# Fillers of half the columns in bank 6 and up to a later time, four result buffers in the first pass, and the place of the later sums split in two

## The chip, the cores and the metric

The kernel runs on one core of one Trainium2 chip. The metric is the device time in microseconds (us) of one execution; the median of the runs counts. The five engines of the core that the text names are TensorE (PE in the profile, with PEld for its weight loads), VectorE (DVE), ScalarE (ACT), GpSimd (POOL) and SyncE (SP), whose queue issues the DMA transfers.

## The reference

Attention over a window of 128 positions with a linear bias, in 8 batches of 8 heads (576 positions, 64 dimensions each), and a gated feed-forward layer on its 4608 tokens. All inputs are float32.

```python
scores = scale * np.matmul(q, k.transpose(0, 1, 3, 2))
rel = pos[:, None] - pos[None, :]
bias = slopes[:, None, None] * (-np.abs(rel).astype(np.float32))[None, :, :]
mask = (rel >= 0) & (rel < window)
scores = np.where(mask, scores + bias[None], -1000000000.0)
scores = scores - np.max(scores, axis=-1, keepdims=True)
attn = np.exp(scores)
attn = attn / (np.sum(attn, axis=-1, keepdims=True) + 1e-09)
x = np.matmul(attn, v)                         # then laid out as (4608, 512)
gate = 1.0 / (1.0 + np.exp(-(x @ w_gate)))     # w_gate, w_val: 512 x 1536
val = x @ w_val
out = gate * val @ w_out                       # 1536 x 512
```

## The kernel before, in words

The work is in three passes over the tokens. The first pass lies beside the attention: as soon as the tokens of a block of 512 are there, `ffn` computes 2 of the 12 chunks of 128 hidden units for them and stores the partial result to DRAM (`part`). Two more passes, with 5 chunks each, read the partial results back and add to them (`ffn2`, tokens in blocks of 768). Every operand of the feed-forward layer is split into a high and a low part of the type fp32r, and a product is three matmuls (high x high, low x high, high x low). The float32 weights are decoded from integer words by ScalarE (L299) and VectorE (L300, L303) before they are split (`prepare`, `prepare2`).

Attention goes through the eight PSUM banks `mm[0]` to `mm[7]` so: scores (L386) into banks 2 to 5, masking there by VectorE (L399), bias and maximum (L407), exponentials on ScalarE (L410), normalisation (L430, L431), transposes (L435) into bank 6, copies `both` from there (L181), a selection on GpSimd (L446), values (L472) into bank 7 and, for the last 64 columns, into the tail of bank 6, and copies `xt` of both (L181). The first pass has banks 0 and 1 for itself until the attention is nearly over, and all eight in its last two blocks.

The order of each engine is not the order of the code: every operation is put into a graph with an engine, a planned cost and keys that it reads and writes, and `order` plays a list schedule. An operation of the kind `copy` or `minus` may go to one of two engines. Where the planner sees a gap ahead of an operation on PE that starts before `WARM`, it fills it with calls of `warm` (L246), matmuls whose result nobody reads, as many as the gap holds at a price written into `order`. The tile framework adds the waits that the use of the same tile asks for; an operation of ScalarE on bank 6 thus waits for an earlier matmul into bank 6, whatever its columns.

`project_out` multiplies the hidden units by `w_out` (L559), and ScalarE copies the result into a buffer `ob` (L567) from which SP's queue stores it; in the later passes VectorE adds the partial result `pi` instead (L564). In the second and third pass a chunk is seven products (L660) of sums of the token block, `combo(0)` to `combo(6)`, with sums of the weights; the banks are combined through `a1`, `u2` and `p5` (L667, L675). The sums of the tokens take the place `area`, in which the first pass has its split tokens and its weights, all but the lower half of `w_out`: that has a place of its own, `area_o`, which the sum `s1` takes over. `follow` puts an empty operation into the graph that makes the listed keys wait for each other at the change of passes.

## Time and profile before

| | |
|---|---|
| runs | 1047.24, 1048.8 and 1049.0 us, median 1048.8 |
| profiled execution | 1052.11 us, of which 1050.4 are its span |
| PE busy | 1030.6 us, 98% of the span |
| VectorE, ScalarE, GpSimd busy | 731.5, 529.0, 110.7 us |
| granted clock of TensorE, mean | 0.997 |
| first pass and attention | 0 to about 360 us |
| second and third pass | from about 360 us to the end |

Times in the rows are counted from the first instruction of the span. A granted clock of 1.00 is TensorE's higher level of 2.4 GHz, 0.50 the lower of 1.2 GHz. A float32 matmul of the program shows as two records in the trace.

### The profile page before, as it was taken

The numbers are of one execution on the slowest core, as the hardware profiler recorded it, in microseconds if no ns is written. First come the engines' busy times: TensorE is split into PE (matmuls) and PEld (weight loads), VectorE is DVE, ScalarE is ACT, GpSimd is POOL, SyncE is SP. The second block draws the span as 40 slices with busy tenths as digits, with TensorE's granted clock in tenths as the row PEclk, the third lists the DMA queues.
The fourth block names the chain that finished last, engine by engine and source line by source line (L and its number), as shares of the span: only waits on it lengthen the run. The fifth ranks groups of instructions, "written<-read, shape, count | busy, mean of one in ns | idle before, by whom it ended". The sixth has DMA issues, their size and how long they took to land.

```text
span 1050.4 us, 17342 instructions
## 1 busy us (share of the span) xinstructions
PE 1030.6 (98%) x6024; PEld 915.9 (87%) x6024; DVE 731.5 (70%) x2045; ACT 529.0 (50%) x1466; POOL 110.7 (11%) x205
## 2 busy tenths in 40 slices
PE   9899999999998999999999999999999999999998
PEld 7577778878877898989999998989898999999896
DVE  8998788798878776474747475999647474747352
ACT  6898688787855542433424152645243342415140
POOL 2333233343310000000000000010000000000000
PEclk9999999999999999999999999999999999999999
DMA  8758576857455715032220405362403223050303
GB/s 290 247 191 278 187 236 212 303 169 263 162 177 181 238 61 158 23 100 81 86 95 26 155 1 181 100 200 82 151 31 106 75 68 113 9 172 1 120 1 100
DMA packets 74727, 142.68 MB, mean 136 GB/s; under 512 B 7312, under 2 KB 30224, under 8 KB 74640
## 3 DMA queue, kind: packets, MB, share of 16 engines
q1 hardware_dynamic: 74640, 141.58, 40.7%
q8 instruction: 47, 0.77, 0.3%
q14 instruction: 40, 0.33, 0.1%
HBM read 103.81 MB, written 37.75 MB: 135 GB/s over the span
## 4 chain that ended last, share of the span: by engine, by line
PE 90%; DVE 5%; ACT 3%; DMA 1%; issue 1%; POOL 0%; ACTq 0%; DVEq 0%; POOLq 0%
PE mm L660 42%; PE mm L559 26%; PE mm L522 8%; PE mm L472 5%; PE mm L386 5%; PE mm L435 3%; ACT pb L410 1%; DVE first L190 1%; PE mm L246 1%; DMA wraw<-in_moe_w_out_dram 1%; DMA wraw<-in_moe_w_gate_dram 1%; ACT both L181 1%; DVE wbits L303 0%; DVE mm L399 0%; DVE w2s L190 0%
## 5 line engine op out<-in xcount | busy, mean ns | idle before, releaser
L660 PE MATMUL mm<-later,w2s 128*128 128x384 f32 x2160 | 386.6, 335 | 1.6 <-ACT later L181 1.3
L660 PEld LDWEIGHTS mm<-later,w2s 128*128 128x128 f32 x2160 | 377.3, 188 | 3.4 <-ACT later L181 1.7
L559 PE MATMUL mm<-w2o,hidden 128*128 128x512 f32 x1080 | 249.2, 390 | 0.0
L559 PEld LDWEIGHTS mm<-w2o,hidden 128*128 128x128 f32 x1080 | 202.4, 188 | 40.8
L671 ACT ACTIVATE sg<-mm 128x384 f32<-128x384 f32 x120 | 59.0, 492 | 149.2 <-PE mm L660 99.4
L181 ACT COPY a<-mm 128x384 f32<-128x384 f32 x60 | 28.8, 480 | 196.1 <-PE mm L660 192.8
L446 POOL TENSOR_SCALAR_AFFINE_SELECT pt<-both 128x384 f32<-128x384 f32 x192 | 103.7, 563 | 183.2 <-ACT both L181 160.7
L522 PE MATMUL mm<-first 128*128 128x512 f32 x432 | 113.2, 405 | 2.6 <-ACT ob L567 2.5
L564 DVE SCALAR_TENSOR_TENSOR ob<-mm,pi 128x512 f32<-128x512 f32 x72 | 49.5, 689 | 73.3 <-PE mm L559 40.0
L522 PEld LDWEIGHTS mm<-first 128*128 128x128 f32 x432 | 78.9, 191 | 20.2 <-ACT ob L567 4.1
L667 DVE TENSOR_TENSOR mm<-mm,a 128x384 f32<-128x384 f32 x60 | 33.7, 564 | 79.3 <-PE mm L660 79.3
L410 ACT ACTIVATE pb<-pb,st 128x128 f32<-128x128 f32 x216 | 84.6, 398 | 3.1 <-DVE st L407 2.9
L660 PE MATMUL mm<-xc,w2s 128*128 128x384 f32 x360 | 73.0, 337 | 0.4 <-DVE p L667 0.4
L472 PEld LDWEIGHTS mm<-pt,vr 128*64 128x64 f32 x832 | 61.2, 137 | 12.6 <-issue 9.5
L472 PE MATMUL mm<-pt,vr 128*64 128x256 f32 (+2 forms) x832 | 67.4, 306 | 0.6 <-POOL pt L446 0.6
L660 PEld LDWEIGHTS mm<-xc,w2s 128*128 128x128 f32 x360 | 63.6, 188 | 1.7 <-DVE p L667 0.7
L181 ACT COPY both<-mm 128x384 f32<-128x384 f32 x94 | 44.8, 477 | 34.3 <-PE mm L435 22.4
L399 DVE COPY_PREDICATED mm<-early_h,mm 128x256 f32<-128x256 int32 (+1 forms) x144 | 49.1, 392 | 9.7 <-PE mm L386 9.3
L386 PE MATMUL mm<-kr,qr 64*128 64x256 f32 (+1 forms) x396 | 55.3, 383 | 0.0
L559 PE MATMUL mm<-first,early_h 128*128 128x512 f32 x144 | 52.4, 409 | 2.2 <-DVE early_h L190 2.0
L407 DVE CUSTOM_DVE_ANT_0 pb<-mm,early_h 128x128 f32<-128x128 f32 x216 | 51.3, 280 | 0.0
L667 DVE TENSOR_TENSOR mm<-mm,u 128x384 f32<-128x384 f32 x60 | 33.9, 565 | 19.8 <-PE mm L660 19.8
(112 smaller groups left out, 1287.7 us busy)
## 6 DMA issues: line engine op xcount, KB each, us to landing
part<-ob SPq DMA_DIRECT2D x72, 256.0 KB, 3.7
pi<-part SPq DMA_DIRECT2D x72, 256.0 KB, 3.4
later_xr<-xs SPq DMA_DIRECT2D x16, 768.0 KB, 5.1
kr<-in_k_dram SPq DMA_DIRECT2D x21, 576.0 KB, 5.4
vr<-in_v_dram SPq DMA_DIRECT2D x32, 288.0 KB, 3.4
xs<-xt SPq DMA_DIRECT2D x32, 288.0 KB, 3.0
out_dram<-ob SPq DMA_DIRECT2D x36, 256.0 KB, 2.1
qr<-in_q_dram SPq DMA_DIRECT2D x21, 320.0 KB, 5.8
```

The source lines that it names most:

```text
L181: g.add("ACT", act_cost(n, psum), lambda: nc.scalar.copy(out(), src()), reads, writes, want, release=release, ways=[("DVE", dve_cost(n, ps ...
L386: nc.tensor.matmul(sp[bank_of(r, a)][:, a % 2, lo:], qraw(u)[rows, i // 2], kraw(u)[rows, (i - 1) * P + lo:(i + 1) * P], start=True, stop= ...
L407: g.add("DVE", 0.21, lambda: nc.vector.tensor_tensor_reduce(pb()[:, e], sp[b][:, a, P:], relm[u.p][:, w], op0=ALU.add, op1=ALU.min, scale= ...
L410: g.add("ACT", 0.39, lambda: nc.scalar.activation(pb()[:, e], pb()[:, e], AF.Exp, bias=st()[:, e:e + 1], scale=-1.0, accum_out=st()[:, 3 + ...
L446: nc.gpsimd.affine_select(pt(u)[:, f0:f0 + 2 * n - 1:2, :], both(), [[0, n], step], cmp, 0.0, base=0, channel_multiplier=mult)
L472: nc.tensor.matmul(to()[e * D:(e + 1) * D, a - e * S - t0:b - e * S - t0], vraw(u)[:, c], seen, start=first, stop=last, skip_group_check=True)
L522: nc.tensor.matmul(mm[s], w.tile(kind, wi)[:, i, c * P:(c + 1) * P], x()[:, c, :], start=(k == 0 and c == 0), stop=(k == 2 and c == KC - 1))
L559: nc.tensor.matmul(mm[s], hcol(x, i, w is w1)[:, ts], w.tile("o", wi)[:, i, :], start=(i == 0 and k == 0), stop=(i == n - 1 and k == 2))
L564: g.add("DVE", dve_cost(DM, psum=True), lambda: nc.vector.scalar_tensor_tensor(ob(), mm[s], 0.5, pi(), op0=ALU.mult, op1=ALU.add), [("mm", ...
L660: nc.tensor.matmul(mm[b][:, 0:N2], w.tile2(i, wp)[:, wk, c * P:(c + 1) * P], combo(k, xp)[:, c], start=(start and c == 0 and j == 0), stop ...
L667: g.add("DVE", dve_cost(N2, psum=True), lambda: nc.vector.tensor_tensor(o(), bk(b)(), a(), op=ALU.add), [("mm", b), *reads] if okeys else ...
L671: g.add("ACT", act_cost(N2, psum=True), lambda: nc.scalar.activation(sg[h](), bk(b)(), AF.Tanh, scale=0.5), [("mm", b)], [("sg", h)], F)
```

## The change

Five things change. The planner fills gaps up to 80 us where it stopped at 30, and counts a filler at 0.13 us (0.23 ahead of 5 us) where it counted 0.25 (0.45). The filler has 64 moving columns and writes the last 64 columns of bank 6, where it had 128 and wrote the first 128 of bank 1. The first pass uses four buffers `ob`, of which the third and the fourth share the place of the `pi` buffers of the later passes. The area is shorter by one weight half: both halves of the first pass's `w_out` are now in `area_o`, which later takes `combo(5)`, while `s1` moves to the pool of the later weights; and the empty operation at the change of passes is split, so that the sums 0 to 4 wait for the tokens and the two input weights, and `combo(5)` for `w_out`. Last, `a1` and `u2` have one buffer where they had two.

```diff
--- before.py
+++ after.py
@@ -44,7 +44,7 @@
 SLACK = 1.0
 W0, WSTEP = 20.0, 2.0
 SWITCH = 0.36
-WARM = 30.0
+WARM = 80.0
 YIELD = {"DVE": 0.1, "POOL": 0.0}
 NRAW = 2
 
@@ -119,7 +119,7 @@
                 mode = o.mode
                 o.start += SWITCH / 2
             if o.eng == "PE" and o.start < WARM:
-                gap = (o.start - free["PE"] - 0.2) // (0.25 if free["PE"] > 5.0 else 0.45)
+                gap = (o.start - free["PE"] - 0.2) // (0.13 if free["PE"] > 5.0 else 0.23)
                 if gap > 0:
                     self.fill.append((free["PE"] + 0.01, int(gap)))
             wait.remove(o)
@@ -243,13 +243,13 @@
 
     def warm(n):
         for _ in range(n):
-            nc.tensor.matmul(mm[1][:, 0:P], ident, ident, start=True, stop=True)
+            nc.tensor.matmul(mm[6][:, NB - D:], ident, ident[:, 0:D], start=True, stop=True)
 
     g.warm = warm
 
 
 
-    AREA = 2 * KC * NB + 5 * FC1 * DM
+    AREA = 2 * KC * NB + 4 * FC1 * DM
     area = lambda a, n, name="first": T(moe, name, [P, AREA], F32R, tag="area")[:, a:a + n]
 
     class First:
@@ -257,7 +257,8 @@
 
         def tile(self, kind, part_):
             a = 2 * KC * NB + (2 * "gvo".index(kind) + part_) * FC1 * DM
-            t = area(a, FC1 * DM) if a < AREA else T(moe, "first_o", [P, FC1 * DM], F32R, tag="area_o")
+            size = FC1 * DM
+            t = area(a, size) if kind != "o" else T(moe, "first_o", [P, 2 * size], F32R, tag="area_o")[:, part_ * size:(part_ + 1) * size]
             return t.rearrange("p (i f) -> p i f", i=FC1)
 
         def keys(self, i):
@@ -547,10 +548,11 @@
 
     def project_out(r, at, h, w, col, F):
         n, last = len(w.fcs), w.fcs[-1] == NFC - 1
-        s, o, ts = bank(), outs[0] % 2, slice(at, at + P)
+        many = 4 if w is w1 else 2
+        s, o, ts = bank(), outs[0] % many, slice(at, at + P)
         outs[0] += 1
         pi = lambda: T(moe, f"pi{o}", [P, DM], F32)
-        ob = lambda: T(moe, f"ob{o}", [P, DM], F32)
+        ob = lambda: T(moe, f"ob{o}", [P, DM], F32) if o < 2 else T(moe, f"ob{o}", [P, DM], F32, tag=f"pi{o - 2}")
         if w.fcs[0]:
             move(pi, lambda: part[r], [("part", r)], [("pi", o)], F, 256)
         for i in range(n):
@@ -579,7 +581,12 @@
 
     def combo(k, part_):
         n = 4 * N2
-        tile_ = area(k * n, n, "later") if k < ROOM else T(pools["w2"], f"xc{k}", [P, n], F32R)
+        if k < ROOM:
+            tile_ = area(k * n, n, "later")
+        elif k == ROOM:
+            tile_ = T(moe, "later_o", [P, 2 * FC1 * DM], F32R, tag="area_o")[:, 0:n]
+        else:
+            tile_ = T(pools["w2"], f"xc{k}", [P, n], F32R)
         return tile_.rearrange("p (h c t) -> p h c t", h=2, c=2)[:, part_]
 
 
@@ -621,7 +628,7 @@
                      [("xs", b, p) for p in range(NPAIR)], [("xr", k, (h, a % N2 > 0)) for k in range(2)], F, 2 * (e - a))
                 a = e
         xk = {(h, k): [("xr", k, (h, e)) for e in range(2)] for h in range(2) for k in range(2)}
-        s1 = lambda: T(moe, "later_s1", [P, FC1 * DM], F32, tag="area_o")[:, 0:2 * N2].rearrange("p (c t) -> p c t", c=2)
+        s1 = lambda: T(pools["w2"], "xsum1", [P, 2, N2], F32)
         s2 = lambda: T(moe, "xsum", [P, 2, N2], F32)
         m = 2 * N2
 
@@ -648,8 +655,8 @@
         def chunk(i):
             bx, by, bz = bank(), bank(), bank()
             e = i % 2
-            small = lambda x: T(pools["w2"], f"{x}{e}", [P, N2], F32)
-            a1, u2, p5 = (lambda x=x: small(x) for x in ("a1", "u2", "p5"))
+            small = lambda x: T(pools["w2"], x, [P, N2], F32)
+            a1, u2, p5 = (lambda x=x: small(x) for x in ("a1", "u2", f"p5{e}"))
             sg = [lambda h=h: T(moe, f"sg{h}", [P, NB], F32)[:, 0:N2] for h in range(2)]
             bk = lambda b: (lambda: mm[b][:, 0:N2])
 
@@ -679,7 +686,7 @@
                 minus(lambda: hcol("hl", i, False)[:, h * N2:(h + 1) * N2], val, lambda: as32(hi()), N2, keys + [("hh", i, h)],
                       [("hl", i, h)], F, psum=psum)
 
-            ka, ku, kp = (("a1", e), ("u2", e), ("p5", e))
+            ka, ku, kp = ("a1", "u2", ("p5", e))
             product(0, bx, True, 0)
             copy(a1, bk(bx), N2, [("mm", bx)], [ka], F, psum=True)
             product(3, bz, True, 3)
@@ -753,7 +760,10 @@
             def follow(keys):
                 g.add("PY", 0.0, lambda: None, [], keys, FIRST)
 
-            follow(tenants(0, 2 * AREA) + ["w2pool", "s1"] + [("xc", k, j) for k in range(7) for j in range(2)])
+            follow(tenants(0, AREA) + [("xc", k, j) for k in range(ROOM) for j in range(2)])
+            follow(tenants(AREA, 2 * AREA) + [("xc", ROOM, j) for j in range(2)])
+            follow(["w2pool", "s1", "a1", "u2", ("p5", 0), ("p5", 1)] + [("xc", k, j) for k in range(ROOM + 1, 7) for j in range(2)])
+            follow([("ob", o) for o in range(4)] + [("pi", o) for o in range(2)])
             follow([("xr", c, e) for c in range(KC) for e in range(2)] + [("xr", k, (h, e)) for k in range(2) for h in range(2) for e in range(2)])
             follow([(x, i, h) for x in ("hh", "hl") for i in range(FC2) for h in range(2)] + ["w2pool"])
         for t in range(NT2):
```

In the changed file L299 is L300, L386 is L387, L435 is L436, L472 is L473, L522 is L523, L559 is L561, L567 is L569 and L660 is L667.

The order of PE near the start, behind the first scores. `mm1` and `mm6` are PSUM banks, `ident` is the unit matrix. Before:

```order
L246 MATMUL mm1_141<-ident_71 128x128 x12
L435 MATMUL mm6_146<-ident_71,early_h2_148 128x128 [waits DVE_49] x3
L246 MATMUL mm1_141<-ident_71 128x128 x2
L386 MATMUL mm2_142<-kr0_150,qr0_152 128x256
L386 MATMUL mm4_144<-kr1_166,qr1_168 128x128 [waits DMAHW6_49,DMAHW5_49]
L386 MATMUL mm2_142<-kr1_166,qr1_168 128x256
```

After:

```order
L246 MATMUL mm6_146<-ident_71 128x64 x24
L436 MATMUL mm6_146<-ident_71,early_h2_148 128x128 [waits DVE_49] x3
L246 MATMUL mm6_146<-ident_71 128x64 x3
L387 MATMUL mm2_142<-kr0_150,qr0_152 128x256
L387 MATMUL mm4_144<-kr1_174,qr1_176 128x128 [waits DMAHW6_49,DMAHW5_49]
L387 MATMUL mm2_142<-kr1_174,qr1_176 128x256
```

The groups of fillers are longer and go to bank 6, into which the transposes between them write too. Over the whole program PE had groups of 8, 12, 2, 9 and 9 calls; it has groups of 16, 24, 3, 18, 18 and 17, the last behind the transposes of `early_h2` and in front of the values (L472) that start at 34.55 us in the trace before.

The order of ScalarE in the last block but two of the first pass, at the result copies. Before:

```order
L567 ACTIVATE ob0_1184<-mm0_140 128x512 [waits DMAHW6_49,PE_49]
L567 ACTIVATE ob1_1220<-mm1_141 128x512 [waits DMAHW0_49,PE_49]
L181 CAST w2o0_3755<-wbits1_400 128x512 [waits DVE_49]
L299 ACTIVATE wbits0_364<-wraw1_190 128x512 [waits DMAHW4_49,DVE_49,Activation_49]
L567 ACTIVATE ob0_1184<-mm0_140 128x512 [waits DMAHW5_49,PE_49,Activation_49]
L567 ACTIVATE ob1_1220<-mm1_141 128x512 [waits DMAHW6_49,PE_49,Activation_49]
```

After:

```order
L300 ACTIVATE wbits0_394<-wraw1_198 128x512 [waits DMAHW1_49,DVE_49]
L569 ACTIVATE ob0_1240<-mm0_140 128x512 [waits DMAHW2_49,PE_49,Activation_49]
L569 ACTIVATE ob1_1276<-mm1_141 128x512 [waits DMAHW4_49,PE_49,Activation_49]
L181 CAST w2o0_3814<-wbits1_439 128x512 [waits DMAHW7_49,DVE_49]
L569 ACTIVATE ob2_1345<-mm0_140 128x512 [waits DMAHW6_49,PE_49,Activation_49]
L569 ACTIVATE ob3_1420<-mm1_141 128x512 [waits DMAHW7_49,PE_49,Activation_49]
```

The decode into `wbits0` stood between the second and the third copy; it stands ahead of the first.

The order of PE at the change of passes: the last group of the last block of the first pass and the first products of the second pass. Before:

```order
L559 MATMUL mm7_147<-first_406,early_h0_1002 128x512
L559 MATMUL mm7_147<-first_o_955,early_h0_1002 128x512
L559 MATMUL mm7_147<-first_406,early_h1_1022 128x512
L660 MATMUL mm0_140<-later_3989,w2s00_2670 128x384 [waits Activation_49]
L660 MATMUL mm0_140<-later_3989,w2s01_2735 128x384
L660 MATMUL mm0_140<-later_3989,w2s00_2670 128x384 [waits DVE_49]
```

After, the end of the block before the last:

```order
L561 MATMUL mm7_147<-first_o_998,early_h0_1058 128x512 [waits Activation_49]
L561 MATMUL mm7_147<-first_o_998,early_h0_1058 128x512
L561 MATMUL mm7_147<-first_o_998,early_h1_1078 128x512
L667 MATMUL mm0_140<-later_4006,w2s00_2635 128x384 [waits Activation_49]
L667 MATMUL mm0_140<-later_4006,w2s01_2646 128x384
L667 MATMUL mm0_140<-later_4006,w2s00_2635 128x384 [waits DVE_49]
L667 MATMUL mm0_140<-later_4006,w2s00_2635 128x384
L667 MATMUL mm0_140<-later_4006,w2s01_2646 128x384
L667 MATMUL mm0_140<-later_4006,w2s00_2635 128x384
L561 MATMUL mm4_144<-first_o_998,early_h0_1058 128x512 [waits Activation_49]
```

The first six products of the second pass stood behind all of L559; now the whole last block of L561, whose first row is the last one here, follows on them.

## Rows read from the trace of the kernel before

**Rows 1.** The page: its head, the row of PE in part 1 (busy time, share of the span, instructions), and the shares by engine of the chain that ended last.

```profile
span 1050.4 us, 17342 instructions
...
PE 1030.6 (98%) x6024; PEld 915.9 (87%) x6024; DVE 731.5 (70%) x2045; ACT 529.0 (50%) x1466; POOL 110.7 (11%) x205
...
PE 90%; DVE 5%; ACT 3%; DMA 1%; issue 1%; POOL 0%; ACTq 0%; DVEq 0%; POOLq 0%
```

**Rows 2.** Two stretches: their length, busy time and records of each engine, the granted clock of TensorE, the DMA share and GB/s.

```profile
24.00:80.00 56.00, 50.65 (x398) 37.60 (x397) 52.97 (x266) 51.82 (x209) 20.70 (x36) 1.00 0.65 218
365.00:1050.00 685.00, 680.99 (x3583) 637.40 (x3581) 423.81 (x701) 254.44 (x507) 2.78 (x2) 1.00 0.27 89
```

**Rows 3.** What PE waited for between 20 and 100 us: us in total, times, longest.

```profile
PE mm L435 <- ACT both L181: 4.5, 8, 1.1
```

**Rows 4.** The same between 100 and 366 us.

```profile
PE mm L522 <- ACT ob L567: 2.5, 2, 1.8
PE mm L559 <- DVE early_h L190: 2.0, 2, 1.2
...
PE mm L660 <- ACT later L181: 1.3, 1, 1.3
PE mm L660 <- DVE later L190: 0.4, 1, 0.4
```

**Rows 5.** The two stretches of four microseconds behind late stalls, in the columns of rows 2 (the granted clock stands behind the busy times).

```profile
330.00:334.00 4.00, 4.00 (x12) 3.13 (x11) 2.48 (x5) 0.99 (x2) 0.00 (x0) 0.57 0.80 201
361.00:365.00 4.00, 4.00 (x16) 4.00 (x15) 4.00 (x6) 3.36 (x6) 0.00 (x0) 0.57 0.63 166
```

**Rows 6.** PE in order of time: start, length, line, tiles, shapes, records, and in brackets the idle time before them. L246 is the filler, L435 a group of transposes, L386 scores, L472 values.

```profile
1.42 3.78 PE L246 MATMUL mm<-ident 128*128 128x128 f32 x16 [1.42 <-POOL ident masks.py:199]
...
7.86 2.94 PE L246 MATMUL mm<-ident 128*128 128x128 f32 x24
10.64 0.49 PE L435 MATMUL mm<-ident,early_h 128*128 128x128 f32 x3
...
14.10 2.27 PE L246 MATMUL mm<-ident 128*128 128x128 f32 x18
16.21 0.56 PE L435 MATMUL mm<-ident,pb 128*128 128x128 f32 x3
...
17.24 0.60 PE L386 MATMUL mm<-early_h,early_xr 64*128 64x128 f32 x4
...
21.71 2.17 PE L246 MATMUL mm<-ident 128*128 128x128 f32 x18
...
34.55 1.08 PE L472 MATMUL mm<-pt,vr 128*64 128x256 f32 x6
36.20 1.12 PE L472 MATMUL mm<-pt,vr 128*64 128x256 f32 x8 [0.57 <-POOL pt L446]
```

**Rows 7.** Weight loads (PEld) and matmuls of the filler, loads of L472 (64 columns), with the shortest, median and longest duration in ns; and the first filler matmul of the second stretch in the timeline.

```profile
L246 PEld LDWEIGHTS mm<-ident x80: 186/192/333, 1.4 to 23.5; 128*128 128x128 f32 x80
L246 PE MATMUL mm<-ident x80: 275/275/580, 1.4 to 23.6; 128*128 128x128 f32 x80
...
L472 PEld LDWEIGHTS mm<-pt,vr x832: 132/137/138, 19.3 to 296.7; 128*64 128x64 f32 x167
...
7.86 0.38 PE L246 MATMUL mm<-ident 128*128 128x128 f32 x1
```

**Rows 8.** A weight load of the first scores, with what it waited for.

```profile
6.26 0.29 PEld L386 LDWEIGHTS mm<-kr,qr 64*128 64x128 f32 x2 [0.21 <-DMA kr<-in_k_dram]
```

**Rows 9.** VectorE and ScalarE beside these stretches, in order of time: copy_predicated on the scores (L399), and ScalarE's copies (L181) out of bank 6. The row at 22.18 holds both copies of `xt`; the second is of 64 columns from bank 6.

```profile
12.67 0.43 DVE L399 COPY_PREDICATED mm<-early_h,mm 128x256 f32<-128x256 int32 x1 [1.50 <-PE mm L386]
...
18.44 0.28 DVE L399 COPY_PREDICATED mm<-early_h,mm 128x128 f32<-128x128 int32 x1
...
22.18 0.67 ACT L181 COPY xt<-mm 128x512 f32<-128x512 f32 x2
...
35.09 0.46 ACT L181 COPY both<-mm 128x384 f32<-128x384 f32 x1
```

**Rows 10.** Part 6 of the page, stores of the partial results: issues, KB each, median us from issue to landing.

```profile
part<-ob SPq DMA_DIRECT2D x72, 256.0 KB, 3.7
```

**Rows 11.** Around 327 us: the issue of a `w_out` load on SP's queue, ScalarE's decode (L299) and result copies (L567), and PE behind them.

```profile
321.27 0.33 SPq L186 DMA_DIRECT2D wraw<-in_moe_w_out_dram  x1
...
327.75 0.66 ACT L299 ACTIVATE wbits<-wraw 128x512 f32<-128x512 f32 x1 [4.32 <-DMA wraw<-in_moe_w_out_dram]
328.47 1.24 ACT L567 ACTIVATE ob<-mm 128x512 f32<-128x512 f32 x2
...
329.13 2.40 PE L522 MATMUL mm<-first 128*128 128x512 f32 x7 [1.79 <-ACT ob L567]
```

**Rows 12.** The change of passes: ScalarE's first casts of the sums, PE behind them, and in two successive chunks the product that reads `xc` (L660).

```profile
358.65 1.55 ACT L181 CAST later<-later_xr 128x768 fp32r<-128x768 f32 x2
...
359.53 0.62 PE L660 MATMUL mm<-later,w2s 128*128 128x384 f32 x2 [1.27 <-ACT later L181]
...
382.65 1.22 PE L660 MATMUL mm<-xc,w2s 128*128 128x384 f32 x6
...
389.96 1.23 PE L660 MATMUL mm<-xc,w2s 128*128 128x384 f32 x6
```

**Rows 13.** Part 5 of the page: the copies of `a1`.

```profile
L181 ACT COPY a<-mm 128x384 f32<-128x384 f32 x60 | 28.8, 480 | 196.1 <-PE mm L660 192.8
```

## The prediction

> **What bounds the kernel now.** I read the page's shares first. TensorE (PE) is busy 1030.6 of 1050.4 us and carries 90% of the chain that ended last [rows 1]: the kernel is bound by PE almost everywhere, and from 365 us on there is nothing to gain, 680.99 of 685 us being busy at full clock [rows 2]. A change of buffers can then win only where PE stands still or runs at a lower clock, and it loses wherever it gives PE more to do. So next I asked the trace where PE waits. Between 20 and 100 us it waits mainly for ScalarE's copies `both` (4.5 us in eight waits) [rows 3]; between 100 and 366 us for the result copies `ob` (2.5 us), for `early_h` (2.0) and for the sums of the pass change (1.3 and 0.4) [rows 4]. Two of those stalls are followed by four microseconds at a granted clock of 0.57 [rows 5]: of the two levels, most of that stretch is at 1.2 GHz, and each costs 4 x (1 - 0.57) = 1.72 us on top of its wait. Everywhere else that I asked, the column is 1.00, from 24 to 80 us too [rows 2]. Last comes the filler, read as PE's instructions in order of time [rows 6]. One call of it shows as two records.
>
> **The filler, more calls.** The planner divides a gap by the price of one call; the price goes from 0.25 to 0.13 us (0.45 to 0.23 ahead of 5 us). The order gives 16, 24, 3, 18, 18 and 17 calls, 96 in all, where 8, 12, 2, 9 and 9 stood, 40 in all; the last, in front of `values` near 34.6 us, is new. What a call then costs is the question on which the sign rests. Today a record takes (10.64 - 7.86)/24 = 0.116 us in the second stretch and (16.21 - 14.10)/18 = 0.117 in the fourth, each time up to the transpose behind it [rows 6]. If its 128 moving columns set that, 64 columns take half, 0.058. If the load of its 128 x 128 weights sets it, the price does not fall. Two rows speak on the load. The first filler matmul of a stretch lasts 0.38 us where the median is 275 ns, so it stood 0.10 us for its own weights; and a load of 64 columns shows 137 ns where that of 128 columns shows 192, 55 ns for 64 columns, which makes 0.11 us for 128 [rows 7]. Both come to the 0.11 of a record. Every matmul record has a load record (80 and 80), so each would pay for one. I take 0.117 us a record: the load bounds it.
>
> The Trainium skill, "TensorE: Matmul & The Clock Gate", section "Back-to-back issue gap", gives the gap as N/2.4 + 2.5 ns; with two passes of 64 columns to a record that is an estimate of 56 ns, the halved price, but the section itself says that the formula undercounts at small N for want of the weight loads. By it the sum would be that of rival B; the rows of the loads decide against it here.
>
> **What that adds at the start.** Stretch by stretch, at 0.117 us a record:
> first: 16 more records, but here one took 3.78/16 = 0.236, twice as long [rows 6]. Halved exactly it costs nothing; unhalved 3.8, of which a wait for `kr` behind it (0.21 [rows 8]) would take a little. Nearer to nothing, since the half of 0.236 is still as long as a load: +0.6.
> second: 24 more, +2.8, all on the chain, for PE does nothing else from 7.86 to 10.64 and the scores behind it feed VectorE, which idles 1.50 us for them [rows 9].
> third: 2 more, +0.2.
> fourth: 18 more, 2.1 on PE, but VectorE wants the scores of 17.24 (0.60 long) only at 18.44 [rows 6, 9], so 0.6 is hidden: +1.5.
> fifth: 18 more, 2.1 on PE. It now writes bank 6, from which ScalarE copies the 64-column tail of `xt` (second of the two copies at 22.18 [rows 9]); PE's filler stands ahead of that copy, so it waits until about 21.71 + 36 x 0.117 = 25.9, and what is queued behind it (`both`, the exponentials, a decode) waits too. ScalarE is held about 3.4 us where it was not; part of this is the 2.1 again. Between 2.1 and 3.5 I take +3.0.
> sixth: 34 records, 4.0 us, from about 34.6 to 38.6. PE would have waited for POOL until 36.20, so 2.4 is left on PE; the copy `both` at 35.09, next in ScalarE's queue, reads the same bank and is held 3.5 [rows 6, 9]. Take +3.0.
> Together 11.1. Against it stand the decodes and casts that VectorE and ScalarE can run ahead during the delay, and waits of PE on them that shrink; of PE's 4.5 us I take 2 off. **Start: +9.1**, between 6.5 and 12. More fillers buy no clock after 24 us, where it is 1.00 already.
>
> The Trainium skill, "PSUM — Partial Sum Buffer", section "PSUM bank collisions raise a hardware error", wants engines kept apart by bank, disjoint columns not being enough. That speaks against the filler in bank 6; here the waits in the order keep them apart, and the price is the held copies above. No run here shows a collision.
>
> **Four result buffers.** With two, the third `ob` of a block waits for the store of the first, which lands 3.7 us after its issue (median) [rows 10]. PE waits for `ob` twice, 2.5 us together, of which the longer takes 1.8 [rows 4]; the other, 0.7 in the block at 303 us, is this one: -0.7, or nothing if the copy is late for another reason. The larger stall, 1.79 us at 329.13, is not of the buffers alone: ScalarE stood 4.32 us for a `w_out` load in front of the copies at 328.47 [rows 11]. In the changed order that decode stands ahead of all four copies, with its load issued earlier. If the load is in time, the stall and its 1.72 us of clock go (-3.5); if it is late, four copies wait instead of two. I take -2.1, nearer to the good end, because today the load is issued at 321.27 and the copies need it 6.5 us later, and the order issues it ahead of that: 0 to -3.5. Nothing else changes in the first pass; the copies take the same time on ScalarE as before.
>
> **The split place.** Before, the first sum of the second pass may be written only after the last L559 has read `first_o`. Its cast at 358.65 holds PE for 1.27 us until 359.53 [rows 12], then VectorE for 0.4 more [rows 4], then the clock costs 1.72: 3.4 in all. After, products 0 of the first chunk stand between the last two blocks of L561, and their casts wait only for the projections. The wait goes, if VectorE has the sums in time; VectorE has the gated values and the lower halves to do at the same place, and the single `a1` and `u2` add waits between the copies and the totals. I keep a wait of about 1 us and part of the clock: -2.2, from 0 to -3.4. Later on a chunk takes 389.96 - 382.65 = 7.3 us [rows 12], and the copy of the next `a1` comes a whole chunk after the total that reads this one; that cover hides the missing second `a1` and `u2`, so I cost them at nothing. Without it the 60 copies of `a1`, 28.8 us in all [rows 13], would stand open.
>
> **Sum.** +9.1 - 0.7 - 2.1 - 2.2 = +4.1 us. The profiled execution took 1052.1 us (1050.4 of span and 1.7 around it), 3.3 above the median of 1048.8, so it would come to 1056.2 and the median to 1052.9.
>
> **Rivals.**
> A, the forecast: the load of the weights sets the filler's price. The start between 6.5 and 12 and the late gains between 0 and -7.6 span 1047.7 to 1060.8; without the best corner, which is C, 1049.5 to 1060. The upper end also holds the case that a PE that streams half the time is given the lower clock for part of the start.
> B, on the other side: a record takes 0.058 us. Then each of the five old stretches is as long as now, the new one ends at 36.6, and what is left is ScalarE's copies held behind bank 6: some 1.3 at 22.18 and 1.5 at 35.09, less 0.5 hidden, so +2.3; with the late -5.0 that is -2.7, or 1046.1, faster. The point from which it decides is a price under about 0.08 us a record. For it speaks that the price of 0.116 is just twice 0.058 as well; against it the 0.10 that the first matmul stands.
> C: the load bounds, but the start hides more (6.5) and the late stalls go whole (-7.6): -1.1, 1047.7, no change to be seen. For it, that two of the three late stalls have one known cause each; against it, that VectorE and ScalarE are already full there.
> That the four buffers do nothing is inside A: it is worth 0.7.
>
> **How the numbers follow.** Less than 0.2% (2.1 us) either way is about what a measurement of this kernel can't tell from no change. A gets 0.62, B 0.22, C 0.16. The range has to take in B's centre, so 1045.5 to 1060.0; A alone is 1049.5 to 1060. Faster: most of B, 0.20. Same: C, the low end of A and a little of B, 0.22. Slower: 0.58, the rest of A.
>
> **What would show it.** A filler record's spacing in the second stretch: 0.11 or more (A) or near 0.06 (B). The last score group of the first stretch, now ending near 7.9 us, ends near 8.5; the transposes of 10.64 move to about 14. ScalarE idles 3 us ahead of the `xt` copy and 3 ahead of `both`, released by PE's L246. Then no wait on `ob` before 326 us, a shorter one or none at 329, granted clock 1.00 there, and at the pass change one short wait on VectorE. The prediction is wrong if the filler's spacing halves, if the copies don't wait for it, or if a new wait on `a1` or `u2` shows in every chunk.

## The result, and the profile after

The changed kernel is slower: 1.0097 of the time before, with an interval of [1.0073, 1.0122], which is +10.2 us on 1048.0 (7.7 to 12.8), where 1048.0 is the median of the kernel before with a fourth execution counted. Differences between kernels are given below as such ratios times 1048.0 us; they can stand a microsecond off the difference of two medians. The forecast was slower by 4.1 us, 1052.9 us in a range from 1045.5 to 1060.0; the profiled execution took 1058.42 us and another 1057.86. Two further executions, of 1073.9 and 1074.7 us, are slow ones by their length and are left out of the comparison.

The page of the changed kernel, its head, the row of PE in part 1 and the shares of the chain, to be held against [rows 1]:

```profile
span 1056.7 us, 17665 instructions
...
PE 1042.2 (99%) x6136; PEld 929.3 (88%) x6136; DVE 731.3 (69%) x2031; ACT 531.0 (50%) x1477; POOL 116.4 (11%) x208
...
PE 96%; ACT 2%; DVE 1%; issue 0%; POOL 0%; ACTq 0%; POOLq 0%
```

PE is busy 11.6 us longer than before and its share of the chain grew from 90 to 96%. There is less waiting and more work, and the span is 6.3 us longer than that of the profiled execution before (which, at 1052.1, was itself 4 us above the median).

PE in order of time at the start, the answer to [rows 6]: start, length, line, tiles, shapes, records, and the idle time before them.

```profile
1.42 7.09 PE L246 MATMUL mm<-ident 128*128 128x64 f32 x32 [1.42 <-POOL ident masks.py:199]
8.44 3.79 PE L387 MATMUL mm<-kr,qr 64*128 64x128 f32 x16
12.16 5.64 PE L246 MATMUL mm<-ident 128*128 128x64 f32 x48
17.64 0.50 PE L436 MATMUL mm<-ident,early_h 128*128 128x128 f32 x3
...
21.28 4.23 PE L246 MATMUL mm<-ident 128*128 128x64 f32 x36
25.35 0.50 PE L436 MATMUL mm<-ident,pb 128*128 128x128 f32 x3
...
28.38 2.08 PE L473 MATMUL mm<-pt,vr 128*64 128x256 f32 x26
...
30.77 4.13 PE L246 MATMUL mm<-ident 128*128 128x64 f32 x36
...
47.73 3.91 PE L246 MATMUL mm<-ident 128*128 128x64 f32 x34
...
52.87 1.79 PE L473 MATMUL mm<-pt,vr 128*64 128x256 f32 x20 [0.23 <-POOL pt L447]
```

A filler record takes (17.64 - 12.16)/48 = 0.114 us in the second stretch and 0.113 in the fourth, with half of the columns: the price did not fall. In the first stretch it takes 7.09/32 = 0.222, and the scores behind it 3.79 us where they took 2.79, so they also still ran slowly. Values that began at 19.31 and 36.20 us begin at 28.38 and 52.87: +9.1 and +16.7 us.

The weight loads of the filler (shortest, median, longest in ns), against [rows 7], and the two copies of ScalarE out of bank 6 that now wait for the end of a filler, against [rows 9]:

```profile
L246 PEld LDWEIGHTS mm<-ident x192: 186/192/339, 1.4 to 51.3; 128*128 128x128 f32 x192
```

```profile
34.94 0.21 ACT L181 COPY xt<-mm 128x64 f32<-128x64 f32 x1 [3.61 <-PE mm L246]
...
51.75 0.48 ACT L181 COPY both<-mm 128x384 f32<-128x384 f32 x1 [3.29 <-PE mm L246]
```

A load still takes 192 ns in the median, one for every matmul; in the first stretch the median is 333. The copy of the 64-column tail and the copy `both` were not waiting for PE before; they now stand 3.61 and 3.29 us.

What PE waited for in the first pass after 100 us, against [rows 4], without the transposes; and four stretches with their granted clock (behind the busy times), the last two against [rows 5]:

```profile
PE mm L561 <- ACT early_h L181: 0.7, 1, 0.7
PE mm L561 <- DVE early_h L190: 0.4, 1, 0.4
```

```profile
2.00:8.00 6.00, 6.00 (x30) 6.00 (x30) 3.39 (x15) 0.08 (x1) 0.00 (x0) 1.00 0.92 301
39.00:44.00 5.00, 4.57 (x26) 3.15 (x26) 4.13 (x33) 4.40 (x21) 1.99 (x4) 0.66 0.50 180
330.00:334.00 4.00, 4.00 (x19) 3.31 (x18) 4.00 (x7) 1.62 (x4) 2.03 (x2) 1.00 0.31 117
361.00:365.00 4.00, 4.00 (x20) 3.30 (x19) 4.00 (x7) 2.01 (x3) 0.00 (x0) 1.00 0.02 6
```

The waits on `ob` (2.5 us) and on the first sums (1.3 and 0.4) are gone. The two stretches that stood at 0.57 are at 1.00; instead there is one near 40 us, at 0.66. The first row, from 2 to 8 us, reads 1.00 too, although the records in it stand 0.222 us apart.

PE at the change of passes, against [rows 12], has no idle time left; one block of L561 lies between the first products and the others, as the order says:

```profile
365.40 1.23 PE L667 MATMUL mm<-later,w2s 128*128 128x384 f32 x6
366.47 2.92 PE L561 MATMUL mm<-first_o,early_h 128*128 128x512 f32 x12
369.23 2.96 PE L667 MATMUL mm<-later,w2s 128*128 128x384 f32 x16
```

### The profile page after: what moved, and what is told of

The parts are those of the page before. It is cut to its first block, busy times and chain, and to the rows that moved or that the text cites. A ratio compares the mean times of both kernels' runs of the same rounds, so it can differ in the third digit from the quotient of the medians.

```text
span 1056.7 us, 17665 instructions
## 1 busy us (share of the span) xinstructions
PE 1042.2 (99%) x6136; PEld 929.3 (88%) x6136; DVE 731.3 (69%) x2031; ACT 531.0 (50%) x1477; POOL 116.4 (11%) x208
## 4 chain that ended last, share of the span: by engine, by line
PE 96%; ACT 2%; DVE 1%; issue 0%; POOL 0%; ACTq 0%; POOLq 0%
PE mm L667 42%; PE mm L561 28%; PE mm L523 9%; PE mm L387 6%; PE mm L473 6%; PE mm L436 4%; PE mm L246 2%; ACT both L181 0%; ACT pb L431 0%; DVE first L190 0%; ACT pb L411 0%; ACT early_xr L411 0%; DVE first L182 0%; ACT early_h L411 0%; DVE st L426 0%
## 5 line engine op out<-in xcount | busy, mean ns | idle before, releaser
L667 PE MATMUL mm<-later,w2s 128*128 128x384 f32 x1800 | 332.0, 335 | 0.0
L667 PEld LDWEIGHTS mm<-later,w2s 128*128 128x128 f32 x1800 | 314.7, 188 | 1.1
L561 PE MATMUL mm<-w2o,hidden 128*128 128x512 f32 x1080 | 249.2, 390 | 0.0
L561 PEld LDWEIGHTS mm<-w2o,hidden 128*128 128x128 f32 x1080 | 202.5, 188 | 40.7
L181 ACT COPY a<-mm 128x384 f32<-128x384 f32 x60 | 28.8, 480 | 195.2 <-PE mm L667 194.5
L523 PE MATMUL mm<-first 128*128 128x512 f32 x432 | 111.6, 401 | 0.0
L523 PEld LDWEIGHTS mm<-first 128*128 128x128 f32 x432 | 77.8, 188 | 15.4 <-issue 1.0
L667 PE MATMUL mm<-xc,w2s 128*128 128x384 f32 x360 | 73.0, 338 | 0.0
L473 PEld LDWEIGHTS mm<-pt,vr 128*64 128x64 f32 x832 | 61.3, 137 | 12.6 <-issue 8.8
L667 PE MATMUL mm<-later_o,w2s 128*128 128x384 f32 x360 | 72.3, 335 | 0.0
L473 PE MATMUL mm<-pt,vr 128*64 128x256 f32 (+2 forms) x832 | 67.7, 307 | 0.2 <-POOL pt L447 0.2
L667 PEld LDWEIGHTS mm<-xc,w2s 128*128 128x128 f32 x360 | 63.4, 188 | 1.6 <-DVE p L674 0.7
L667 PEld LDWEIGHTS mm<-later_o,w2s 128*128 128x128 f32 x360 | 63.2, 188 | 0.5 <-ACT u L181 0.5
L181 ACT COPY both<-mm 128x384 f32<-128x384 f32 x95 | 45.2, 476 | 36.2 <-PE mm L436 17.2
L561 PE MATMUL mm<-first_o,early_h 128*128 128x512 f32 x216 | 57.0, 403 | 1.2 <-ACT early_h L181 0.7
L387 PE MATMUL mm<-kr,qr 64*128 64x256 f32 (+1 forms) x396 | 57.3, 396 | 0.0
```

Of the source, the lines that this page charges most:

```text
L181: g.add("ACT", act_cost(n, psum), lambda: nc.scalar.copy(out(), src()), reads, writes, want, release=release, ways=[("DVE", dve_cost(n, ps ...
L387: nc.tensor.matmul(sp[bank_of(r, a)][:, a % 2, lo:], qraw(u)[rows, i // 2], kraw(u)[rows, (i - 1) * P + lo:(i + 1) * P], start=True, stop= ...
L473: nc.tensor.matmul(to()[e * D:(e + 1) * D, a - e * S - t0:b - e * S - t0], vraw(u)[:, c], seen, start=first, stop=last, skip_group_check=True)
L523: nc.tensor.matmul(mm[s], w.tile(kind, wi)[:, i, c * P:(c + 1) * P], x()[:, c, :], start=(k == 0 and c == 0), stop=(k == 2 and c == KC - 1))
L561: nc.tensor.matmul(mm[s], hcol(x, i, w is w1)[:, ts], w.tile("o", wi)[:, i, :], start=(i == 0 and k == 0), stop=(i == n - 1 and k == 2))
L667: nc.tensor.matmul(mm[b][:, 0:N2], w.tile2(i, wp)[:, wk, c * P:(c + 1) * P], combo(k, xp)[:, c], start=(start and c == 0 and j == 0), stop ...
```

## The experiments

The filler and the rest of the change touch different stretches, so the first four runs take them apart.

**The old filler in the changed kernel.**

```diff
-WARM = 80.0
+WARM = 30.0
...
-                gap = (o.start - free["PE"] - 0.2) // (0.13 if free["PE"] > 5.0 else 0.23)
+                gap = (o.start - free["PE"] - 0.2) // (0.25 if free["PE"] > 5.0 else 0.45)
...
-            nc.tensor.matmul(mm[6][:, NB - D:], ident, ident[:, 0:D], start=True, stop=True)
+            nc.tensor.matmul(mm[1][:, 0:P], ident, ident, start=True, stop=True)
```

> The changed kernel with the filler of before (128 columns, bank 1, old prices, until 30 us); the buffers and the split place stay. Theory L (the start costs 16.7 us by the longer filler, and the buffers and the split place win 10.4 us by themselves): the start runs as before, scores at 46.6 are back at 33.3, and the time is 1048.0 - 10.4 = about 1037.6 us, 1.0% under the kernel before. Rival D (part of the late gain only comes because a late start lets loads and decodes run ahead of PE): the late stalls come back in part, and the gain is 5 us or less, 1043 us or more.

Measured: 1042.18 us, ratio 0.9942 [0.9928, 0.9957], a gain of 6.1 us. Two stretches of the filler:

```profile
1.42 3.56 PE L246 MATMUL mm<-ident 128*128 128x128 f32 x16 [1.42 <-POOL ident masks.py:199]
...
8.00 2.95 PE L246 MATMUL mm<-ident 128*128 128x128 f32 x24
```

The start is that of the kernel before, and the late waits stay away: between 100 and 370 us PE has the same two on `early_h` as the changed kernel, 0.7 and 0.4 us, beside those of the transposes. So the buffers and the place win about 6 us by themselves. That is less than the 10.4 that the two traces show between them (+16.7 at 53 us, +6.3 at the end), but not because the gain hangs on a late start, as D has it: the trace of before, at 1052.1 us, had 4 us more to lose than the median. The other half of the comparison is needed to see that.

**The new filler in the kernel before.** The same three lines the other way round, in the kernel before.

> The kernel before with the new filler alone (64 columns into bank 6, new prices, until 80 us). Theory L: +16.7 us at the start and the old stalls at 327 and at the pass change stay, so 1064.7 us. Rival D: the stalls shrink without any change of the buffers, since the loads have 16.7 us more; 1055 to 1060 us.

Measured: 1064.99 us, ratio 1.0156 [1.014, 1.0173], +16.3 us, as L has it. With the -6.1 of the run above this makes +10.2, the measured difference: the two halves add up (each is known to some 1.6 us either way), and D falls. Its profile, PE's filler in the second, fourth and fifth stretch and PE's late waits:

```profile
12.16 10.50 PE L246 MATMUL mm<-ident 128*128 128x64 f32 x48
...
29.24 7.94 PE L246 MATMUL mm<-ident 128*128 128x64 f32 x36
...
44.05 4.13 PE L246 MATMUL mm<-ident 128*128 128x64 f32 x36
...
PE mm L522 <- ACT ob L567: 2.1, 2, 1.4
PE mm L660 <- ACT later L181: 1.3, 1, 1.3
PE mm L559 <- DVE early_h L190: 0.8, 1, 0.8
PE mm L660 <- DVE later L190: 0.4, 1, 0.4
```

The late waits are there: 4.6 us in all, where the profile before has 6.2 [rows 4], with 2.1 on `ob` where it was 2.5 and the same 1.3 at the change of passes. The profiled execution, at 1079.45 us, was 14.5 above the other four, so even some 30 us more for the loads don't remove them. In it records of the second and the fourth stretch took 10.50/48 = 0.219 and 7.94/36 = 0.221 us, twice the price, and only the fifth 4.13/36 = 0.115. The lower speed held until about 40 us there.

**Half of the weights as well.**

```diff
-            nc.tensor.matmul(mm[6][:, NB - D:], ident, ident[:, 0:D], start=True, stop=True)
+            nc.tensor.matmul(mm[6][0:D, NB - D:], ident[:, 0:D], ident[:, 0:D], start=True, stop=True)
```

> The changed kernel whose filler loads 64 columns of weights instead of 128 and so writes 64 partitions; moving columns, bank, counts and places are the same. Theory W (the load of the weights sets the price): a record falls from 0.115 to about 0.06 us, the second stretch from 5.6 to about 2.9 us, the start costs 2 to 4 us instead of 16.7, and the time is 1040 to 1043 us. Rival K (the waits on bank 6 make the loss, not the length of the filler): ScalarE's copies still wait and the time stays above 1052 us. Rival C (the 64 columns set it in some other way, 0.115 us is the floor of a record): no change, 1058 us.

Measured: 1046.22 us, ratio 0.9987 [0.9976, 0.9997]; 0.0110 less than the changed kernel, 11.5 us. Loads of the filler, its first two stretches, and the transposes behind the fifth:

```profile
L246 PEld LDWEIGHTS mm<-ident x192: 133/138/227, 1.4 to 38.7; 128*64 128x64 f32 x192
...
1.42 3.67 PE L246 MATMUL mm<-ident 128*64 128x64 f32 x32 [1.42 <-POOL ident masks.py:199]
...
8.21 3.01 PE L246 MATMUL mm<-ident 128*64 128x64 f32 x48
...
27.14 0.91 PE L436 MATMUL mm<-ident,pb 128*128 128x128 f32 x3 [1.24 <-ACT pb L431]
```

A record falls to 3.01/48 = 0.063 us, and to 3.67/32 = 0.115 in the first stretch. Nothing but the width of the weights, and with it the number of partitions written, is changed, so the load of 128 columns did set the price, at both speeds: W holds, and C falls. The time is 3 us above W's range: a filler of the planned length still holds ScalarE's copies, and PE waits 1.24 us for ScalarE in front of the transposes. Against the kernel with the old filler PE is 2.1 us late there (27.14 against 25.05) and 3.9 behind the sixth stretch (values at 40.19 against 36.32).

**The filler in bank 1.**

```diff
-            nc.tensor.matmul(mm[6][:, NB - D:], ident, ident[:, 0:D], start=True, stop=True)
+            nc.tensor.matmul(mm[1][:, 0:D], ident, ident[:, 0:D], start=True, stop=True)
```

> The changed kernel with its filler in bank 1 instead of bank 6; counts, columns and prices are the same. Theory W: the filler's own time stays (about 12 us at the start) and only the holds of ScalarE's copies in the fifth and sixth stretch go, 3 to 5 us: 1053 to 1055 us. Rival K: the holds are most of the loss, and the time falls to 1045 us or less.

Measured: 1052.73 us, ratio 1.0041 [1.0026, 1.0056]: 0.0056 of the time, 5.9 us, comes from bank 6, the rest stays. W is right, a little short in size; K falls. The second and the sixth stretch are as long as in the changed kernel:

```profile
11.47 5.57 PE L246 MATMUL mm<-ident 128*128 128x64 f32 x48
...
43.43 3.91 PE L246 MATMUL mm<-ident 128*128 128x64 f32 x34
```

Without the held copies the other engines do run ahead here: the values behind the sixth stretch begin 12.7 us later than before (47.27 against 34.55), the first projections (L523) only 11.0 (51.98 against 41.02).

**The prices of before.** The line with 0.25 and 0.45 again, all else as changed.

> The changed kernel with the prices of before (0.25 and 0.45 us a call): 8, 12, 2, 9, 9 and 9 calls of 64 columns into bank 6, until 80 us. Theory W (a record costs 0.117 us, the weight load): the five old stretches are as long as before, the sixth adds 18 records in front of a wait for POOL that was there anyway, and ScalarE's two copies are still held behind bank 6, 2 to 4 us: 1044 to 1046 us, some 3 us over the 1042.2 of the kernel with the old filler. Rival H (a PE that streams only half of each record is given the lower clock for longer, whatever the count): the start loses more than that, 1048 us or more.

Measured: 1050.18 us, ratio 1.0021 [1.0004, 1.0039]. The number of calls (96 instead of 49) is thus worth 0.0076, 8.0 us, but with as many fillers as before plus nine the kernel is still 8.3 us above the one with the old filler. H comes nearer than W. The second and the fourth stretch of the profile:

```profile
9.55 5.38 PE L246 MATMUL mm<-ident 128*128 128x64 f32 x24
...
20.67 2.22 PE L246 MATMUL mm<-ident 128*128 128x64 f32 x18
```

The second stretch runs at 5.38/24 = 0.224 us a record, twice what it took before; only the fourth is at 0.12. With fillers of 128 columns the speed had doubled before the second stretch began (2.95/24 = 0.123).

**No filler.** `WARM = 0.0`.

> The changed kernel without any filler. Theory F (fillers are worth having where they fit the gap: they bring the clock up before the scores need it): the first scores run at the lower clock and the start loses 4 to 10 us against the old filler, 1046 to 1052 us. Rival N (PE waits for loads, VectorE and ScalarE in these gaps anyway, so fillers buy nothing): 1040 to 1042 us, at least as good as the old filler's 1042.2.

Measured: 1047.11 us, ratio 0.9989 [0.9979, 0.9999]: 4.9 us above the kernel with the old filler. F holds. PE's first work with its waits:

```profile
3.61 1.62 PE L387 MATMUL mm<-kr,qr 64*128 64x128 f32 x6 [3.61 <-DMA qr<-in_q_dram]
...
10.99 0.88 PE L436 MATMUL mm<-ident,early_h 128*128 128x128 f32 x3 [1.99 <-DVE early_h L432]
...
17.80 0.48 PE L436 MATMUL mm<-ident,pb 128*128 128x128 f32 x1 [1.09 <-ACT pb L431]
```

The first scores start 1.3 us earlier than with the old filler (3.61 against 4.92), but they and the transposes are slow (0.88 us for three where 0.49 was [rows 6]), and PE waits for VectorE and ScalarE in each gap. The old filler is worth its place.

**The place alone, and the buffers alone.** The kernel with the old filler and `many = 2` in all passes, which keeps the single `a1` and `u2`; and the kernel before with

```diff
-        s, o, ts = bank(), outs[0] % 2, slice(at, at + P)
+        many = 4 if w is w1 else 2
+        s, o, ts = bank(), outs[0] % many, slice(at, at + P)
...
-        ob = lambda: T(moe, f"ob{o}", [P, DM], F32)
+        ob = lambda: T(moe, f"ob{o}", [P, DM], F32) if o < 2 else T(moe, f"ob{o}", [P, DM], F32, tag=f"pi{o - 2}")
...
+            follow([("ob", o) for o in range(4)] + [("pi", o) for o in range(2)])
```

> Old filler, split place, but two result buffers in the first pass as before. Of the 5.5 us that the buffers and the place win together, theory S (the stall at 327 us belongs to the buffers, that at the pass change to the place) leaves about 3: 1044 to 1045.5 us. Rival P (the place moves the order enough to do all of it): 1042 us. Rival Q (the place does nothing, VectorE is late instead): 1047.5 us.

> The kernel before with four result buffers in the first pass and nothing else. Theory S: the waits on the result copies go and the stall at the pass change stays, 2 to 3 us: 1044.5 to 1046 us. Rival P: 1047.5 us. Rival Q: 1042 us.

Measured: 1047.51 us, ratio 1.0001 [0.9991, 1.001], and 1048.25 us, ratio 1.0 [0.9991, 1.0009]. Neither S nor P nor Q: each alone wins nothing, together they win 6.1 us. With the place alone, PE waits for result copies; the last row is ScalarE's third copy of that block:

```profile
PE mm L523 <- ACT ob L569: 2.7, 3, 1.4
...
PE mm L561 <- DVE early_h L190: 1.1, 2, 0.7
PE mm L561 <- ACT early_h L181: 0.7, 1, 0.7
...
304.83 11.17 PE L523 MATMUL mm<-first 128*128 128x512 f32 x48 [1.45 <-ACT ob L569]
...
304.18 0.60 ACT L569 ACTIVATE ob<-mm 128x512 f32<-128x512 f32 x1 [2.88 <-DMA part<-ob]
```

Its waits on `ob` make 2.7 us where they made 2.5 [rows 4], and the one in the block at 303 us grew from 0.7 to 1.45: the third copy stands 2.88 us for the store of an earlier one, the wait that the prediction gave to two buffers, and begins at 304.18 where it began at 303.05. The decode behind the `w_out` load still waits as well, 4.93 us where it waited 4.32 [rows 11]. All waits of the view, without the transposes, are 4.5 us where they were 6.2, so 1.7 should be left as a gain, of which the interval allows 0.9. The 6.2 were read in an execution 4 us above the median, which may have waited longer than most; the rest stays open. With the buffers alone no wait on `ob` is left, and PE comes to the change of passes 4.9 us earlier (at 353.3, where it came at 358.3); there it waits:

```profile
355.15 0.62 PE L661 MATMUL mm<-later,w2s 128*128 128x384 f32 x2 [1.82 <-ACT later L181]
357.57 11.90 PE L661 MATMUL mm<-later,w2s 128*128 128x384 f32 x52 [1.81 <-DVE later L190]
...
355.00:364.00 9.00, 7.04 (x24) 6.73 (x25) 7.73 (x11) 4.89 (x9) 0.00 (x0) 0.62 0.68 218
```

1.82 and 1.81 us where it was 1.27 and 0.37, and the stretch behind them is at a granted clock of 0.62, 9 x 0.38 = 3.4 us, a part of which falls into the second wait. All ten executions list a mean clock of 0.998 or less, where nine of the ten with the place alone list 1.000. So most of the gain has moved to the next wait, which is the one that the split place removes.

**Columns, bank and time of the filler, one at a time.** All three are the kernel with the old filler, with one thing changed: the 128 columns in bank 6; 64 columns in bank 1; until 80 us. In the first the filler writes over 64 columns of the tail in which values stand, so that part of the result is lost and only the time counts.

> The kernel with the buffers and the place of the change and the filler of before (128 columns, old prices, until 30 us), which now writes bank 6 instead of bank 1. Theory B2 (bank 6 costs what ScalarE's copies wait for the filler's end): only the copy behind the fifth stretch is held, about 1.5 us: 1043 to 1044.5 us against 1042.2 with bank 1. Rival R (bank 6 keeps PE from streaming evenly and so keeps the clock low): 1046 us or more, and the second stretch longer than 3.0 us.

> The same kernel with fillers of 64 columns in bank 1, as many as before (8, 12, 2, 9, 9). Theory H (fillers that stream half of the time leave the clock low for longer): the granted clock comes up near 20 us instead of near 5, the second stretch takes about 5 us instead of 2.95, and the time is 1047 to 1050 us. Rival G (with the prices of before and without bank 6 the columns don't matter, because a record takes the time of its weight load either way): 1042 to 1043 us.

> The same kernel with the filler of before, bank 1, but until 80 us: a sixth stretch of 9 calls, 2.1 us, in front of values that wait for GpSimd anyway. Theory W: it is nearly hidden, and the clock is up there already: 1041.5 to 1043.5 us. Rival T (the later time was worth something: without it the stall at 52 us brings the clock down): 1040.5 us or less, and no stretch at a lower clock near 52 us.

Measured: 1043.67 us, ratio 0.996 [0.9945, 0.9975]; 1048.12 us, 1.0001 [0.998, 1.0021]; 1041.88 us, 0.9942 [0.9921, 0.9963]. So at the old number of calls bank 6 costs 1.9 us (B2), the 64 columns 6.2 and the later time nothing (W). Together 8.1, and the kernel with the old prices had lost 8.3; as each of these is known only to some 2 us, the agreement may be chance. In bank 6 the second stretch is as fast as ever, and the wait for ScalarE appears behind the fifth:

```profile
7.62 2.94 PE L246 MATMUL mm<-ident 128*128 128x128 f32 x24
...
25.94 0.91 PE L436 MATMUL mm<-ident,pb 128*128 128x128 f32 x3 [1.24 <-ACT pb L431]
```

The kernel with 64 columns took from 1044.05 to 1053.01 us in its ten executions, where the one with 128 columns stayed between 1041.73 and 1043.45. Its profile is that of the execution at 1044.05, and shows little of the loss:

```profile
1.42 3.68 PE L246 MATMUL mm<-ident 128*128 128x64 f32 x16 [1.42 <-POOL ident masks.py:199]
...
8.88 2.89 PE L246 MATMUL mm<-ident 128*128 128x64 f32 x24
```

A record of the first stretch takes 3.68/16 = 0.230, no less than with 128 columns (3.56/16 = 0.223), and the second stretch is fast here. That the other executions lose their time to a second stretch like that of the run with the prices of before is argued from that run's profile, not seen. The two shortest executions list a mean clock of 0.998 and the eight longer ones 1.000, so what those lose shows in that column as little as the slow start does. The sixth stretch until 80 us costs nothing, since PE waits there anyway:

```profile
34.87 2.17 PE L246 MATMUL mm<-ident 128*128 128x128 f32 x18
```

**The changed kernel again.**

> The changed kernel itself once more, in more executions. Theory H (fillers that stream half of the time bring the clock up late, and at a moment that varies): the times fall into groups, near 1058 us where the clock comes up in the second stretch, and near 1074 us where it stays low until about 40 us, as in the profile of the kernel with the new filler alone; the range over the executions is 10 us or more, where the kernel with the old filler stays within 2 us. Rival X (the longer executions of the changed kernel came from outside of it): all within 3 us of 1058.

Measured: 1059.19 us, from 1058.09 to 1060.87, ratio 1.0104 [1.0087, 1.0121]. X comes nearer: no group near 1074 showed in these four, and what made the two longest executions of the first measurement stays open. The slowdown itself is confirmed. In this profile, of the execution at 1058.09 us, the values behind the sixth stretch begin at 52.22 us, 16.0 late, and the two copies stand 3.59 and 3.29 us, but from 38 to 44 us the granted clock is 1.00: the low stretch near 40 us is no fixed part of the loss.

The best kernel of the study is the changed one with the old filler, until 30 or 80 us: 1042.2 and 1041.9 us, 0.6% under the kernel before and 1.5% under the changed one.

## Why the prediction was right, and where its steps were not

**The sign and its ground** were right. The price of a record was forecast at 0.117 us against 0.058 and is 0.114; that the load of the weights sets it was read from two rows [rows 7] and is shown by the run with half of the weights. B falls with it: its price came true only in that run, and not its sum: the start cost 4.7 us there against B's 2.3, and the late gain was 6.1 against 5.0, so that the 1046.2 us fall near B's 1046.1 by two misses that offset each other.

**The start** was forecast at +9.1 us, between 6.5 and 12. It is +16.3, outside that range, and this is the step that failed. By terms: the first stretch was put at +0.6, "since the half of 0.236 is still as long as a load". It cost 3.3, since a load takes longer there as well: 333 ns, which stood in [rows 7] as the longest of all loads, so that a record takes 0.222. And the scores behind it lost another 1.0 (3.79 against 2.79), which had no term; I had thought of the low speed lasting longer only as an edge of the range. These scores were to end near 8.5 us and ended at 12.2; the transposes came at 17.64, not about 14. Second +2.8: the delay is 7.0 us at 17.64, of which 4.3 come from ahead, so 2.7. Third and fourth 1.7: 2.1 (9.1 at the values of 28.38). Fifth and sixth 6.0: 7.6, with the two holds of ScalarE 3.61 and 3.29 us against my 3.4 and 3.5, and a stretch at 0.66 of the clock (5 x 0.34 = 1.7 us) behind the wait that the first hold made; in the second profile of the changed kernel, without that stretch, it is 6.6 (16.0 at the values of 52.22 less 9.4 at those of 28.73), so this term was about right. The 2 us that I took off for work that runs ahead were not there: the first projections (L523) are 16.7 us late like everything at 53 us. With the filler in bank 1 they were there, 1.7 us (12.7 less 11.0), so it is the copies held in ScalarE's queue that cost them.

**The late gain** was forecast at -5.0 and is -6.1, inside its range. But its parts do not add as the sum has them. Buffers -0.7 and -2.1, place -2.2: alone each is 0.0 within 1 us. With the place alone the waits on `ob` stay; with the buffers alone what they win is lost at the next wait and by the clock behind it; only both together leave PE neither. The clock terms (1.72 us each) were sized from one execution: of the sixty-five executions of the kernel before beside all the runs, 38 list a mean clock of 1.000 (median 1047.4 us) and 27 a lower one (1048.9), so those losses are not in most of them, and are worth some 1.5 us where they are. The stalls alone went to 1.1 us from 6.2 in the profile before [rows 4] and from 4.6 in that of the new filler alone, 3.5 to 5.1 of the 6.1; where the rest lies is not shown. The missing second `a1` and `u2` show in no wait, as forecast at nothing.

**The total** lies in the range because that had been drawn up to 1060: the start was 7.2 us short, the late gain 1.1, and 4.1 + 7.2 - 1.1 is the measured 10.2. That it lies there is in part luck: the measured start with the forecast late gain comes to 1048.8 + 16.3 - 5.0 = 1060.1 us, beyond the range.

## What to carry to other kernels

A filler must be priced by what it costs in the trace, not by its columns: with full weights and few columns the load sets the price, and the filler outgrows the gap it was counted for. Write it where nobody waits for the same bank or tile. When several waits stand in a row, a change that removes one of them can measure as nothing and still be part of a gain, so try them together before dropping one.

## What the runs showed of the hardware

A weight load slows down with the lower of TensorE's levels, as the moving columns do. Two groups of eight loads of 128 columns for the scores of the changed kernel, the first at a granted clock of 1.00, the second at 0.50 (from 40 to 43 us):

```profile
L387 PEld LDWEIGHTS mm<-kr,qr x8: 183/187/187, 38.0 to 38.6; 64*128 64x128 f32 x8
...
L387 PEld LDWEIGHTS mm<-kr,qr x8: 286/334/336, 40.4 to 41.5; 64*128 64x128 f32 x8
```

The filler's loads at the start last as long as the second group, 333 ns, and its records stand 0.222 us apart there and 0.114 later with 128-column weights, 0.115 and 0.063 with 64. But the clock that the profile gives for the first microseconds is 1.00, so at the start the length of the loads and the spacing of the records tell more.

Fillers of 64 columns with full weights brought the faster spacing later and less surely. With 128 columns it was there in the second stretch of every profile (which began from 7.6 to 8.3 us). With 64 columns and full weights it was there in a second stretch that began at 8.88 us, at 11.47, and twice at 12.16; once it came only after a second stretch that began at 9.55, and in one profile not before about 40 us. With 64 columns and weights of 64 it was there at 8.21. What sets the moment is not shown.
